# One hand-written work list of a convolution and SwiGLU kernel: a split sum and a tap of VectorE moved behind a step that they stood ahead of, and ten stores moved forward

## The chip, the cores and the metric

The kernel runs on one core of one Trainium2 chip. A core has four engines that compute, each with its own in-order list of instructions: TensorE (PE in the profile, its weight loads PEld), VectorE (DVE), ScalarE (ACT) and GpSimd (POOL). SyncE (SP) computes nothing; here it asks for nearly all DMA transfers, one after the other. The engines meet only through semaphores. The metric is device time in microseconds (us) of one execution, and the median over several runs is what counts.

## The reference

The computation has two layers, all in float32 (x comes in as float32, the weights as float64 words that the kernel converts itself):

```python
# x (8, 4096, 192), weight (8, 7): a causal depthwise convolution of 7 taps, one softmaxed filter per head of 24 columns
w = softmax(weight, axis=-1)
out[b, s, h, g] = sum_k w[h, k] * x_pad[b, s + k, h, g]
# then, on the 32768 rows of 192 columns:
xn  = x / sqrt(mean(x * x) + 1e-6) * rms_g
g   = xn @ w_gate            # 192 x 1536
val = xn @ w_val             # 192 x 1536
y   = (g * sigmoid(g) * val) @ w_out   # 1536 x 192
```

## The kernel before

The 32768 rows are worked in 32 pairs (0 to 31) of 1024 tokens. From pair 2 on, one pair goes through these stages:

- Loads: SyncE brings x of the pair, one transfer a head (`Sld.h`, line 174), into the one buffer `xh`; a pair that starts a sequence has one more small transfer for the zeros ahead of it (line 178).
- Convolution: tap 0 is a scaled copy on ScalarE (`Acv0`, line 470), taps 1 to 6 are multiply-adds on VectorE (`Vcv1` to `Vcv6`, line 474). They all work in place on the one buffer `y`.
- Normalisation (`Asq`, `Vred`, `Gpow`, `Vbc`, `Gmul`), eight stores into a scratch tensor (`Spl`, line 1098) and transfers back in token order into `xb` (`Sft`, line 676).
- Splitting: `Vx`, `An`, `Vl`, `Vd` make block sums of the tokens and cut each of five operands into three parts of fewer bits (lines 868, 705, 854, 856). Word `Vd.4` makes the third part of the fifth operand.
- Gate and value products: 68 products (line 948), each of six matmuls of 64x512, with weights from a ring of 12 places that SyncE refills from DRAM (line 822), 48 refills a pair. Eleven places have the name `ring`, and the twelfth lies in `part`. A place is asked for again as soon as its last product has read it.
- Between them ScalarE takes the silu (`Ag`, line 1031), VectorE multiplies (`Vm`, line 1038) and adds accumulators in PSUM (`Vf`, line 1025).
- Output: 42 steps on TensorE (line 976) into three accumulators X, Y and Z. `VC21` and `VC22` (line 1055) add an accumulator to a copy of another; `VT11`, `VT12`, `VT21` and `VT22` (line 991, two transposes each) turn the four quarters into `o_sb`; ten transfers `Sst0.0` to `Sst1.4` (line 1087) store them, `Sst0` for the first half of the tokens and `Sst1` for the second. A store needs both quarters of its half. The ten have 96, 96, 128, 32 and 32 KB for each half, all in runs of 64 floats, which is 256 bytes.

Nothing plans this order when the kernel is built: it is written out by hand as lists of words. `run` (line 1301) goes through a list and issues each word on the engine that its first letter names (A, V, G, S); `p3` issues the next three entries of the pair's list `LINE` (products, then steps) on TensorE. A plus behind a word means the next pair, two the one after it, a minus the pair before. So each list joins the tail of one pair with the body of the next and with what is got ready for later pairs. `FIRST` (line 115) serves pair 1, `SECOND` (line 98) pair 2, and `ORDER` (line 81) each of the pairs 3 to 31. Each engine runs its instructions in the order in which they were issued, and SyncE is no exception: a transfer whose data or place isn't ready holds up every transfer behind it.

Around the joint of pairs 1 and 2 the words stand so. `FIRST` ends with `VC21 p1 Vh4.4`, then the split sum and the tap, `Vd.4+` (pair 2) and `Vcv4++` (pair 3). (`Vl.2+` between them issues nothing, since `FIRST` has the same word earlier and `ahead_done`, line 1316, leaves out the second.) `SECOND` begins with the first two products of pair 2, `VC22-` and `VT11-` of pair 1, and `p6-`: the last six steps of pair 1. These write into accumulator X, which `VC22-` reads, and so can't start before it. At its other end `SECOND` has `Acv0++ p1 VC22 Vd.4+ Vcv4++ p5 VC21`: tap 0 and tap 4 of pair 4 ahead of `VC21`, which frees the accumulator that the first product of pair 3 goes into.

Of the kernel before, what the change touches and what calls it, by code (L numbers as in the profile page):

```python
# [20 lines left out]
def kernel(  # L21
# [75 lines left out]
    )  # L97
    SECOND = (
# [15 lines left out]
    )  # L114
    FIRST = (
# [14 lines left out]
    )  # L130
    LINE = (
# [1223 lines left out]
```

## Time and profile before

| | |
|---|---|
| median of 3 runs | 2451.31 us (2450.36 to 2458.17) |
| the profiled execution's own time | 2452.15 us |
| its span on the core | 2450.4 us |
| PE busy | 2429.1 us (99% of the span) |
| DVE busy | 2090.1 us (85%) |
| mean DMA rate | 176 GB/s |

The profile holds one execution. Its page gives busy times; the view of waits says which engine stood idle and what ended it; the timeline lists instructions in order of time, neighbours of one kind merged; the chain of waits is the work that ended last, followed back; the view of windows gives busy time and granted TensorE clock between two times. In a timeline row stand the start, the length, the engine, the line of the kernel, the operation, out<-in, the shapes, the count and, in brackets, the idle time before it and what ended it. SPq rows are SyncE's issues of DMA transfers, with the time in which SyncE was held in them.

### The profile page before, as it was taken

Reading aid. Unit: us, or ns where it says so; the run is one execution under the profiler, and the core shown is the slowest. Engines: PE = TensorE matmul, PEld = TensorE weight load, DVE = VectorE, ACT = ScalarE, POOL = GpSimd, SP = SyncE. Lnnn points to the kernel's source line nnn. Section 1 sums busy time; section 2 is a strip of 40 time slices with the busy share of each in tenths; the row PEclk is TensorE's granted clock in tenths of the full one; section 3 lists DMA queues with packets and bytes.
Section 4 is the critical chain, followed back from the end, with each engine's and each line's share of the span. In section 5 each row is a group of like instructions: output and inputs, shape, how many; then the busy total and the mean of one; then the engine's idle time right before and its main releaser. Section 6 shows DMA issues by size and latency. Waiting matters only on the chain.

```text
span 2450.4 us, 69381 instructions
## 1 busy us (share of the span) xinstructions
PE 2429.1 (99%) x29136; PEld 1979.6 (81%) x29136; DVE 2090.1 (85%) x2702; ACT 1033.3 (42%) x1431; POOL 565.3 (23%) x482
## 2 busy tenths in 40 slices
PE   8999999999999999999999999999999999999998
PEld 5647788888888888888788888888888788888786
DVE  8688888898888899888898888898888998888974
ACT  6443344444444443444443444433444443444432
POOL 0542122211222211222212222112222112222111
PEclk9999999999999999999999999999999999999999
DMA  7374688777787677787677786777786777876753
GB/s 153 61 212 133 156 197 207 180 170 174 173 205 198 172 179 172 174 214 194 167 178 168 184 213 185 171 176 171 190 210 183 170 174 174 198 201 177 177 157 83
DMA packets 716392, 430.55 MB, mean 176 GB/s; under 512 B 510330, under 2 KB 702386, under 8 KB 716082
## 3 DMA queue, kind: packets, MB, share of 16 engines
q1 hardware_dynamic: 712336, 425.21, 70.9%
q8 instruction: 230, 3.77, 0.7%
q10 hardware_dynamic: 3746, 0.92, 0.2%
q14 instruction: 80, 0.66, 0.1%
HBM read 366.96 MB, written 58.98 MB: 174 GB/s over the span
## 4 chain that ended last, share of the span: by engine, by line
PE 95%; DMA 1%; DVE 1%; POOL 1%; SPq 1%; issue 0%; ACT 0%; DVEq 0%; ACTq 0%; POOLq 0%
PE ps L948 57%; PE ps L976 35%; PE ps L1135 2%; SPq L174 0%; PE ps L920 0%; DMA ht<-in_moe_w_val_dram 0%; POOL ht L1003 0%; POOL part L799 0%; DVE ht L1003 0%; DMA x<-in_x_dram 0%; DMA wd<-part 0%; DMA xh<-in_x_dram 0%; SPq L258 0%; DMA ht<-in_moe_w_gate_dram 0%; DVE y L474 0%
## 5 line engine op out<-in xcount | busy, mean ns | idle before, releaser
L948 PE MATMUL ps<-part,ring 64*128 64x512 f32 x11160 | 1307.8, 387 | 3.6 <-DVE tt L1055 3.6
L948 PEld LDWEIGHTS ps<-part,ring 64*128 64x128 f32 x11160 | 1117.0, 184 | 158.8 <-issue 6.3
L1031 ACT ACTIVATE tt<-ps 128x512 f32<-128x512 f32 x744 | 441.3, 598 | 685.4 <-PE ps L948 618.3
L1038 DVE TENSOR_TENSOR ht<-ps,tt 128x512 f32<-128x512 f32 x744 | 498.8, 687 | 209.5 <-ACT tt L1031 201.2
L976 PE MATMUL ps<-ht,wo_sb 128*32 128x384 f32 (+2 forms) x7272 | 429.4, 380 | 2.6 <-DVE tt L1055 2.5
L976 PE MATMUL ps<-ht,x 128*32 128x256 f32 (+2 forms) x6696 | 411.0, 379 | 0.4 <-POOL ht L1003 0.3
L976 PEld LDWEIGHTS ps<-ht,wo_sb 128*32 128x32 f32 x7272 | 319.0, 110 | 99.4 <-issue 12.5
L976 PEld LDWEIGHTS ps<-ht,x 128*32 128x32 f32 x6696 | 291.7, 110 | 88.2 <-issue 0.8
L474 DVE SCALAR_TENSOR_TENSOR y<-xh,tp,y 128x1536 f32<-128x1536 f32 x186 | 338.3, 1819 | 7.8 <-ACT y L470 7.5
L503 POOL TENSOR_SCALAR r<-r 128x8 f32<-128x8 f32 x31 | 6.1, 197 | 1436.2 <-DVE r L498 1436.0
L1025 DVE TENSOR_TENSOR ps<-ps,tt 128x1024 f32<-128x1024 f32 x210 | 258.7, 1232 | 37.7 <-ACT tt L705 24.9
L705 ACT COPY ps<-ps 128x1024 f32<-128x1024 f32 (+1 forms) x151 | 134.0, 887 | 277.1 <-PE ps L948 126.9
L1003 POOL TENSOR_TENSOR hs<-ht 128x512 f32<-128x512 f32 x120 | 155.2, 1294 | 169.1 <-DVE ht L1038 127.8
L705 ACT COPY tt<-ps 128x384 f32<-128x384 f32 (+1 forms) x182 | 151.6, 833 | 86.9 <-PE ps L976 76.8
L705 ACT CAST part<-tt 128x1024 fp32r<-128x1024 f32 x60 | 62.8, 1046 | 288.7 <-DVE tt L868 288.7
L1003 DVE TENSOR_TENSOR ht<-ht 128x512 f32<-128x512 f32 x252 | 169.7, 705 | 4.7 <-PE ps L976 4.6
L1003 POOL TENSOR_TENSOR ht<-ht 128x512 f32<-128x512 f32 x120 | 154.0, 1294 | 2.3
L976 PE MATMUL ps<-hs,x 128*32 128x128 f32 (+2 forms) x2232 | 143.9, 379 | 0.0
L948 PE MATMUL ps<-part,part 64*128 64x512 f32 x912 | 129.8, 386 | 0.0
L976 PEld LDWEIGHTS ps<-hs,x 128*32 128x32 f32 x2232 | 103.7, 110 | 25.5
L856 DVE SCALAR_TENSOR_TENSOR part<-part,xb 128x1024 fp32r<-128x1024 f32 x87 | 106.5, 1224 | 0.0
L854 DVE TENSOR_TENSOR part<-xb,part 128x1024 fp32r<-128x1024 f32 x87 | 103.9, 1223 | 0.0
(137 smaller groups left out, 1627.6 us busy)
## 6 DMA issues: line engine op xcount, KB each, us to landing
ring<-wd SPq DMA_DIRECT2D x1326, 192.0 KB
xb<-xd SPq DMA_DIRECT2D x60, 512.0 KB
xd<-xh SPq DMA_DIRECT2D x240, 96.0 KB
part<-wd SPq DMA_DIRECT2D x114, 192.0 KB
xh<-in_x_dram SPq DMA_DIRECT2D x192, 105.0 KB
xb<-xd SPq DMA_DIRECT2D x60, 256.0 KB
out_dram<-o_sb SPq DMA_DIRECT2D x126, 96.0 KB
out_dram<-o_sb SPq DMA_DIRECT2D x62, 128.0 KB
```

The lines of the kernel that those rows point to most:

```text
L474: nc.vector.scalar_tensor_tensor(out=y, in0=xk, scalar=w, in1=y, op0=ALU.mult, op1=ALU.add)
L503: nc.gpsimd.tensor_scalar(out=r, in0=r, scalar1=s / D, scalar2=s * 1e-6, op0=ALU.mult, op1=ALU.add)
L705: nc.scalar.copy(out=dst, in_=src)
L854: e.tensor_tensor(out=split_of(g, 1).bitcast(F32R), in0=src, in1=high, op=ALU.subtract)
L856: nc.vector.scalar_tensor_tensor(out=split_of(g, 2).bitcast(F32R), in0=high, scalar=1.0 + SPLIT, in1=src, op0=ALU.mult, op1=ALU.subtract,)
L948: nc.tensor.matmul(out=self.both(j, c)[:, h, :], lhsT=left[HALF[h]], rhs=right[HALF[h]], start=(first and q == 0), stop=True, skip_group_c ...
L976: nc.tensor.matmul(out=self.acc(b)[i * Q : (i + 1) * Q, at : at + n], lhsT=left, rhs=cols, start=fresh, stop=True, skip_group_check=True, ...
L1003: engine[eng].tensor_tensor(out=dst, in0=a, in1=b, op=op)
L1025: nc.vector.tensor_tensor(out=self.both(j, c), in0=self.both(j, "b"), in1=s5, op=ALU.add)
L1031: nc.scalar.activation(out=tt[:, t, :], in_=self.both(j, c)[:, 0, :], func=AF.Silu)
L1038: nc.vector.tensor_tensor(out=self.hv(j, "abcd".index(c)), in0=self.both(j, c)[:, 1, :], in1=tt[:, t, :], op=ALU.mult,)
L1135: nc.tensor.matmul(out=bank(h, bks[h])[:], lhsT=wf[HALF[h], AT[h][k], u * NF + f, :], rhs=xb[HALF[h], g, k, :], start=(k == 0), stop=(k == ...
```

## The change

Only the end of `FIRST` and the list `SECOND` change, so one joint and one pair out of 32. The split sum `Vd.4` of pair 2 goes from ahead of `VC22-` to behind `VT11-` and the word `p6-`. The tap `Vcv4` of pair 3 goes from the same place to behind the fifteenth product of pair 2, just ahead of `Vmb.1`. The word `Vl.2` goes along and issues nothing in either kernel. The ten stores of pair 1 were asked for behind products 13, 14, 15, 55, 57, 60, 61, 65, 65 and 65 of pair 2; now they are asked for behind products 4, 4, 4, 7, 8, 9, 11, 12, 15 and 17. On TensorE, ScalarE and GpSimd the order of instructions stays the same; VectorE has the two instructions moved, and SyncE the stores.

```diff
     SECOND = (
-        "p2 VC22- VT11- p6- VT22- VT21- Vcv5+ VT12- Af1.0 p2 Aga.1 p1 Vma.1 Vl.4 p1 Aga.0 p1",
-        "Af3.0 Vma.0 p4 Vf4.0 p1 Agb.1 p1 Sst0.4- p1 Sst0.2- p1 Sst1.4- Vmb.1 p2 Vf5.0 Agc.0",
+        "p2 Vl.2 VC22- VT11- p6- Vd.4 VT22- VT21- Vcv5+ VT12- Af1.0 p2 Aga.1 Sst0.4- Sst0.2-",
+        "Sst1.4- p1 Vma.1 Vl.4 p1 Aga.0 p1 Sst0.3- Af3.0 Vma.0 p1 Sst1.1- p1 Sst0.0- p2 Vf4.0",
+        "Sst0.1- p1 Agb.1 Sst1.0- p3 Vcv4+ Vmb.1 Sst1.2- p2 Vf5.0 Agc.0 Sst1.3- p1 Vmc.0",
...
-        "Sst0.3- Gh3.0 Spl.6+ Vmd.4 p1 Gh3.1 Vmb.4 p1 Sst1.1- p1 Sft.0+ Af3.5 Sft.2+ p1",
-        "Sft.4+ Gh1.2 p1 Sst0.0- p1 Vf4.5 Sld.4++ Sst0.1- p2 Sft.5+ Aga.5 Vma.5 Sld.3++ p1",
-        "Agc.3 p1 Vf5.5 Sst1.0- Gh3.3 Sst1.2- Gh1.4 Sst1.3- Vh3.2 p1 Sld.7++ Vmc.3 p2 Vf6.5",
+        "Vmd.3 p2 Gh1.0 Agc.4 Spl.3+ Vmc.4 p1 Spl.0+ Agd.4 p1 Af1.5 Gh1.3 Agb.4 Gh3.0 Spl.6+",
+        "Vmd.4 p1 Gh3.1 Vmb.4 p1 p1 Sft.0+ Af3.5 Sft.2+ p1 Sft.4+ Gh1.2 p1 p1 Vf4.5 Sld.4++",
+        "p2 Sft.5+ Aga.5 Vma.5 Sld.3++ p1 Agc.3 p1 Vf5.5 Gh3.3 Gh1.4 Vh3.2 p1 Sld.7++ Vmc.3",
...
     FIRST = (
...
-        "VC21 p1 Vh4.4 Vl.2+ Vd.4+ Vcv4++",
+        "VC21 p1 Vh4.4",
```

19 rows, old and new, of the table SECOND are left out of this document.

## The prediction

> **What bounds the kernel now.** I read the page first, then the waits of TensorE, then the timeline at the two longest ones, then the chain of waits and windows by pair.
>
> ```profile
> PE 2429.1 (99%) x29136; PEld 1979.6 (81%) x29136; DVE 2090.1 (85%) x2702; ACT 1033.3 (42%) x1431; POOL 565.3 (23%) x482
> PE ps L948 <- DVE tt L1055: 3.6, 1, 3.6
> PE ps L976 <- DVE tt L1055: 2.5, 1, 2.5
> PE ps L222 <- DMA tt<-in_weight_dram: 2.1, 1, 2.1
> ```
>
> TensorE is the bound: it is busy for 99% of the span, and in the whole span it waits longer than 2.1 us only twice, each time once and each time for line 1055, the sums `VC22` and `VC21`. Both lie in the stretch that `SECOND` orders. The other 29 pairs have no such wait, so only these two, and what hangs on them, are there to be won. The first:
>
> ```profile
> 208.49 1.66 PE L948 MATMUL ps<-part,ring 64*128 64x512 f32 x12
> 208.61 0.69 DVE L1003 TENSOR_TENSOR ht<-ht 128x512 f32<-128x512 f32 x1 [0.67 <-PE ps L976]
> 209.22 1.22 DVE L856 SCALAR_TENSOR_TENSOR part<-part,tt 128x1024 fp32r<-128x1024 f32 x1
> 210.36 1.81 DVE L474 SCALAR_TENSOR_TENSOR y<-xh,tp,y 128x1536 f32<-128x1536 f32 x1
> 212.09 0.55 DVE L1055 TENSOR_TENSOR tt<-ps,tt 128x384 f32<-128x384 f32 x1
> 212.56 0.64 DVE L991 STREAM_TRANSPOSE o_sb<-ps 128x256 f32<-128x256 f32 x2
> 212.69 4.11 PE L976 MATMUL ps<-ht,wo_sb 128*32 128x384 f32 x72 [2.53 <-DVE tt L1055]
> 216.73 8.47 PE L948 MATMUL ps<-part,ring 64*128 64x512 f32 x72
> 216.87 0.65 DVE L991 STREAM_TRANSPOSE o_sb<-ps 128x256 f32<-128x256 f32 x2 [0.94 <-PE ps L976]
> ```
>
> The reader is to see the queue on VectorE: `Vh4.4` ends, then come `Vd.4` (209.22), `Vcv4` (210.36) and only then `VC22` (212.09), while TensorE has done its two products by 210.15 and stands for 2.53 us. The second wait is at the joint of pairs 2 and 3, and the chain of waits shows what leads up to it:
>
> ```profile
> 278.65 0.89 SPq L174
> ...
> 284.09 4.71 DMA xh<-in_x_dram
> ...
> 289.06 1.58 ACT y L470
> 290.67 1.82 DVE y L474
> 292.49 0.48 DVE tt L1055
> 293.01 48.23 PE ps L948 x408
> ```
>
> SyncE asks for the last of the x loads of pair 4 at 284.09; it lands 4.71 us later, then tap 0, tap 4 and `VC21` follow one by one, and TensorE goes on at 293.01, 4.2 us after the landing. The windows show what that idle time brings behind it:
>
> ```profile
> 208.49:293.01 84.52, 78.35 (x986) 65.17 (x984) 66.40 (x87) 31.50 (x42) 16.48 (x14) 1.00 0.65 161
> 293.01:369.12 76.11, 76.00 (x912) 67.15 (x912) 65.44 (x83) 31.52 (x42) 16.48 (x14) 0.98 0.76 179
> 443.31:517.30 73.99, 73.99 (x915) 63.83 (x914) 64.76 (x83) 31.45 (x42) 16.47 (x14) 1.00 0.77 184
> 289.30:293.00 3.70, 0.07 (x2) 0.00 (x0) 2.33 (x3) 1.34 (x1) 0.00 (x0) 1.00 0.00 0
> 293.30:296.70 3.40, 3.40 (x18) 2.68 (x18) 3.40 (x6) 1.00 (x1) 0.00 (x0) 0.50 0.22 58
> ```
>
> The first three are whole pairs, from the first product of one to that of the next; the third number from the right is the granted clock. An undisturbed pair takes 73.99 us. Pair 3 takes 76.11: it has no wait inside, but right behind the 3.64 us of idleness the clock is 0.50 for 3.4 us. So the second wait costs 3.64 and then another 2.1. Behind the 2.53 us wait the clock stays at 1.00.
>
> **The first two edits: `Vd.4` and `Vcv4` from ahead of `VC22`.** Without them `VC22` starts when `Vh4.4` lets go of VectorE, at 209.22. From its start to TensorE's it took 212.69 - 212.09 = 0.60 us, so the six steps are free at 209.82. TensorE's products end at 210.15. The wait goes whole, with 0.33 us to spare: -2.53.
>
> What is late next? `Vd.4` follows the two transposes of `VT11` and ends near 211.4; its reader is the thirteenth product, ten products of 0.7 (8.47 for twelve) behind the six steps, so near 221: some 9 us of cover hide it. `VT12` waits for the six steps (the 0.94 us above); VectorE has 1.14 us more to do ahead of it, so it comes 0.2 us later behind them, and an accumulator free that much later is hidden by ScalarE's copy and the products ahead of its next use. For `Vcv4`'s new place the trace has a stand-in: in pair 3 another tap stands there (301.89), between the sum `Vf4.0` and the multiply `Vmb.1`.
>
> ```profile
> 301.89 1.81 DVE L474 SCALAR_TENSOR_TENSOR y<-xh,tp,y 128x1536 f32<-128x1536 f32 x1
> 223.83 0.69 DVE L1038 TENSOR_TENSOR ht<-ps,tt 128x512 f32<-128x512 f32 x1 [1.07 <-ACT tt L1031]
> 225.24 1.23 DVE L1025 TENSOR_TENSOR ps<-ps,tt 128x1024 f32<-128x1024 f32 x1 [0.72 <-PE ps L948]
> 227.97 0.69 DVE L1038 TENSOR_TENSOR ht<-ps,tt 128x512 f32<-128x512 f32 x1 [0.73 <-ACT tt L1031]
> ```
>
> Pair 3 has no TensorE wait there. In pair 2 the same stretch has 1.07 + 0.72 + 0.73 = 2.52 us of VectorE idleness, more than the tap's 1.81. Its price lies between 0 and 1.81 (no cover at all); I take 0, from the pair that does it.
>
> **The ten stores.** Where they stood:
>
> ```profile
> 224.97 0.38 SPq L1087 DMA_DIRECT2D out_dram<-o_sb  x1
> 226.46 1.33 SPq L1087 DMA_DIRECT2D out_dram<-o_sb  x2
> 228.63 0.32 SPq L822 DMA_DIRECT2D part<-wd  x1
> 254.63 2.05 SPq L1087 DMA_DIRECT2D out_dram<-o_sb  x1
> 258.47 0.42 SPq L1087 DMA_DIRECT2D out_dram<-o_sb  x1
> 262.25 0.45 SPq L1087 DMA_DIRECT2D out_dram<-o_sb  x1
> 264.42 2.24 SPq L1087 DMA_DIRECT2D out_dram<-o_sb  x1
> 273.57 2.44 SPq L1087 DMA_DIRECT2D out_dram<-o_sb  x3
> 281.77 3.16 SPq L174 DMA_DIRECT2D xh<-in_x_dram  x4
> DMA packets 633, 0.16 MB, mean 161 GB/s; under 512 B 630, under 2 KB 633, under 8 KB 633
> 235.92 0.86 PE L948 MATMUL ps<-part,part 64*128 64x512 f32 x6
> ```
>
> Seven of them hold SyncE for 2.05 + 0.42 + 0.45 + 2.24 + 2.44 = 7.60 us between 254 and 276, a stretch in which SyncE issues without a pause and at the end of which stand the x loads. Taken out, they bring those loads forward by at most 7.60. If the DMA engines are what holds SyncE, the gain is what these save: the seven move 32 + 4*96 + 128 + 32 = 576 KB, 2304 runs of 256 bytes; between 276 and 277, where such runs are nearly all there is, the trace counts 633 packets (the row above), so 2304/633 = 3.6 us. If the refills in between, which wait for TensorE, set SyncE's pace, it is 0; but its rows follow each other without a pause, so that end is far. SyncE is held in some issues (2.05 and 2.24 where a free one takes 0.38 to 0.45) and goes at its own pace in others, so both limits work in turn, and I take some 5.
>
> What is needed? TensorE reaches the joint 2.53 earlier, and SyncE's stream, tied to TensorE by the refills, comes earlier with it. For no wait at all the last x load must land 3.64 us earlier still. That is just the smaller of the two limits, so the second wait goes, or all but a few tenths of it: -3.64. Its half clock goes with it: -(76.11 - 73.99) = -2.1.
>
> At their new places the stores cost SyncE time among the refills. The three early ones took 0.38 and 0.67 each, so ten take 4 to 7 us, and in the 12 us of the first 17 products nine refills at 0.32 take 3 more: there is room. The first one also waits for `VT12`, near 215, when no refill is due: the next place is let go by the fifth product, after it. The tightest cover I can show is that of the twelfth place: asked for at 228.63, read by the product at 235.92, 7.3 us later, of which landing takes some of the 2 to 5 us that DMAs take here. That leaves 2 to 5 us for refills delayed by stores. I take 0 and keep 2 as the bad end.
>
> Sum: -2.53 - 3.64 - 2.1 = -8.3 us, from 2452.15 of this execution to 2443.9. The execution shown lies 0.84 above the median, so against 2451.31 it is 2443.0. Pair 2 took 84.52 - 73.99 = 10.5 us more than an undisturbed one, of which the six steps are 4.0 (212.69 to 216.73) and the two waits 6.2, so at most 0.3 more is to be had: own range 2442.0 to 2444.3.
>
> The Trainium skill (TensorE: Matmul & The Clock Gate, section Part 1: The HAM clock gate) says that the array falls to half clock once it was idle for a whole window of about 3.4 us, and is back after as long a busy one; the trace agrees, with 3.64 us idle, then 0.50 for 3.4 us, and no drop behind 2.53. By that rule even a remaining wait of 3 us would cost only itself.
>
> **The rivals.** First, the loads don't come early enough. For it speaks that the smaller limit, 3.6 us, is just what is needed, and that refills stand between the loads. A remaining wait of 1 to 2.5 us without half clock gives 2444.0 to 2445.5; if all of it stays, with the half clock, only the first 2.53 is won: 2448.8. Second, the first wait gets a successor, at `VT12` or at `Vcv4`'s new place, and up to 1.81 comes back: 2444.8. Pair 3 speaks against it. Third, the other side: the stores hold up the refills behind them. At the price of the late ones (2.05 and 2.24 each) ten take some 21 us; SyncE has 12 - 3 = 9 free in that stretch and the cover is about 4, so TensorE would stand for 8 us, with 2.1 of half clock behind it: 10.1 against a gain of 8.3, so 2453.1. It decides from about 2 us a store; a store at 2.7 us would make it 2460. Against it: early in pair 2 stores took 0.38 to 0.67, since no block transfers of tokens run there. The Trainium skill (DMA: Bandwidth & Descriptors, section Specifications) speaks for it: it asks for runs of at least 512 bytes, with a read-modify-write below; no run here separates that from the 633 packets a us.
>
> **How the numbers follow.** The forecast has 0.63, the late loads 0.25, a successor 0.06, held refills 0.06. What a measurement of this kernel can tell from no change is about 0.3%, 7.4 us, and the forecast is only 0.9 beyond it. Of the first case 0.61 is faster, and of the second 0.03, where less than 0.9 us of the wait stays; the rest of both and the third count as the same, as does 0.02 of the last, whose 0.04 above 2458.7 is slower: 0.64, 0.32 and 0.04. The range takes in the first three cases with a little scatter: 2441.4 to 2449.3.
>
> **What would show it.** First wait: no idle time of TensorE ahead of the steps near 210, and `VC22` right behind `Vh4.4`. Tap: `Vcv4` ahead of `Vmb.1` with no TensorE wait for the next pairs of products. Second: the x loads of pair 4 end near 279 on SyncE, no wait at the joint near 287, and a granted clock of 1.00 in pair 3, which then takes 74.0 us. The prediction is wrong if TensorE waits for a refill in the first 30 products, or if the wait for line 1055 stays with more than 1 us.

## The result, and the profile after

| | before | after |
|---|---|---|
| median of 11 runs, us | 2453.72 (2450.36 to 2458.50) | 2445.48 (2443.56 to 2449.13) |
| ratio of the two | | 0.9965, 95% interval 0.9956 to 0.9974 |
| profiled execution, us (span) | 2452.15 (2450.4) | 2447.03 (2445.2) |

The changed kernel is faster by 0.35%, just beyond the 0.3% that the prediction took for the least that a measurement of this kernel can tell from no change. Both intended waits are gone. The waits of the changed kernel have no line for 1055 any more, and a 2.6 us entry for line 1003, which lies ahead of pair 2 and has its own paragraph below. The first line here is from the page, the others are from the view of waits (columns: us in total, times, longest):

```profile
PE 2427.2 (99%) x29136; PEld 1978.5 (81%) x29136; DVE 2089.3 (85%) x2702; ACT 1034.0 (42%) x1431; POOL 565.7 (23%) x482
PE ps L976 <- DVE ht L1003: 2.6, 2, 1.4
PE ps L222 <- DMA tt<-in_weight_dram: 2.1, 1, 2.1
```

The timeline of the changed kernel at the joint of pairs 1 and 2:

```profile
210.05 1.65 PE L948 MATMUL ps<-part,ring 64*128 64x512 f32 x12
210.17 0.69 DVE L1003 TENSOR_TENSOR ht<-ht 128x512 f32<-128x512 f32 x1 [0.67 <-PE ps L976]
210.78 0.55 DVE L1055 TENSOR_TENSOR tt<-ps,tt 128x384 f32<-128x384 f32 x1
211.25 0.64 DVE L991 STREAM_TRANSPOSE o_sb<-ps 128x256 f32<-128x256 f32 x2
211.64 4.11 PE L976 MATMUL ps<-ht,wo_sb 128*32 128x384 f32 x72
211.81 1.18 DVE L856 SCALAR_TENSOR_TENSOR part<-part,tt 128x1024 fp32r<-128x1024 f32 x1
221.60 1.81 DVE L474 SCALAR_TENSOR_TENSOR y<-xh,tp,y 128x1536 f32<-128x1536 f32 x1
```

`VC22` (210.78) stands right behind `Vh4.4`, the six steps follow the two products at 211.64 with no idle time, and the split sum (211.81) and the tap (221.60) stand at their new places. The same execution's stores and last x loads on SyncE, and the start of pair 3:

```profile
216.49 1.72 SPq L1087 DMA_DIRECT2D out_dram<-o_sb  x3
...
226.94 1.32 SPq L1087 DMA_DIRECT2D out_dram<-o_sb  x2
...
274.99 3.17 SPq L174 DMA_DIRECT2D xh<-in_x_dram  x4
286.62 0.55 DVE L1055 TENSOR_TENSOR tt<-ps,tt 128x384 f32<-128x384 f32 x1
...
288.29 0.96 PE L948 MATMUL ps<-part,ring 64*128 64x512 f32 x6
```

The ten stores are asked for between 216.49 and 228.26. `VC21` (286.62) is done 1.1 us before TensorE comes to the product that needs it. The windows of the changed kernel, pairs 2 and 3 (columns as in the prediction, the third number from the right is the granted clock):

```profile
210.05:288.29 78.24, 78.24 (x987) 64.53 (x985) 67.26 (x87) 31.43 (x42) 16.53 (x14) 1.00 0.69 174
288.29:362.23 73.94, 73.94 (x915) 63.84 (x913) 64.76 (x83) 31.44 (x42) 16.52 (x14) 1.00 0.75 184
```

Against 84.52 and 76.11, pair 2 is 6.28 shorter and pair 3 2.17, together 8.45 us, where the prediction had 8.3. The two profiled executions differ by only 5.12 because this one lost 3.3 us elsewhere. 1.56 of it is lost before pair 2 begins (210.05 against 208.49), at two waits in a part of `FIRST` that the change doesn't touch:

```profile
194.80 1.51 PE L976 MATMUL ps<-ht,x 128*32 128x384 f32 x24 [1.35 <-DVE ht L1003]
197.57 1.81 PE L976 MATMUL ps<-ht,x 128*32 128x384 f32 x28 [1.26 <-DVE ht L1003]
```

The other thirteen profiles of this study, among them a second one of the changed kernel, start pair 2 between 207.64 and 208.94. The remaining 1.7 are stalls of 0.2 to 1 us at scattered places of the later pairs. Their cause isn't known.

### The profile page after: what moved, and what is told of

Same layout as the page of the kernel before. It is cut to its first block, busy times and chain, and to the rows that moved or that the text cites. A ratio compares the mean times of both kernels' runs of the same rounds, so it can differ in the third digit from the quotient of the medians.

```text
span 2445.2 us, 69382 instructions
## 1 busy us (share of the span) xinstructions
PE 2427.2 (99%) x29136; PEld 1978.5 (81%) x29136; DVE 2089.3 (85%) x2702; ACT 1034.0 (42%) x1431; POOL 565.7 (23%) x482
## 3 DMA queue, kind: packets, MB, share of 16 engines
q1 hardware_dynamic: 712336, 425.21, 70.7%
## 4 chain that ended last, share of the span: by engine, by line
PE 97%; DVE 1%; DMA 1%; SPq 1%; issue 0%; ACT 0%; DVEq 0%; ACTq 0%
PE ps L948 57%; PE ps L976 35%; PE ps L920 2%; PE ps L1135 2%; SPq L174 1%; DMA ht<-in_moe_w_val_dram 0%; DVE part L854 0%; DMA x<-in_x_dram 0%; DVE ht L1003 0%; DMA xh<-in_x_dram 0%; DMA ht<-in_moe_w_gate_dram 0%; SPq L258 0%; DVE part L856 0%; DVE y L474 0%; DVE ht L1038 0%
## 5 line engine op out<-in xcount | busy, mean ns | idle before, releaser
L976 PEld LDWEIGHTS ps<-ht,x 128*32 128x32 f32 x6696 | 298.4, 110 | 86.5 <-DVE ht L1003 3.2
L976 PE MATMUL ps<-hs,x 128*32 128x256 f32 (+2 forms) x2232 | 145.2, 379 | 0.0
```

The costliest lines, as they stand in the source:

```text
L976: nc.tensor.matmul(out=self.acc(b)[i * Q : (i + 1) * Q, at : at + n], lhsT=left, rhs=cols, start=fresh, stop=True, skip_group_check=True, ...
```

## The experiments

All the kernels below do the whole computation. Times in the table count from the first product of pair 2; "landing" is the arrival of the last x load of pair 4 as the trace has it. Pair 2 is the time to the first product of pair 3, pair 3 that from there to the first of pair 4.

| run | profiled us | pair 2 | pair 3 | landing | wait ahead of the six steps | wait at the joint | half clock |
|---|---|---|---|---|---|---|---|
| before | 2452.15 | 84.52 | 76.11 | 80.31 | 2.53 | 3.64 | behind the joint |
| b_again (before) | 2450.09 | 82.54 | 74.61 | 77.98 | 2.54 | 0 | in the six steps |
| after | 2447.03 | 78.24 | 73.94 | 70.69 | 0 | 0 | none |
| a_again (after) | 2443.75 | 78.20 | 73.95 | 70.62 | 0 | 0 | none |
| e1_vector | 2445.57 | 78.54 | 74.55 | 74.34 | 0 | 0.24 | none |
| e1_second (same) | 2443.72 | 78.80 | 74.51 | 74.59 | 0 | 0.50 | none |
| e2_stores | 2448.10 | 81.73 | 74.12 | 75.99 | 2.53 | 0 | none |
| e3_queue | 2450.54 | 84.49 | 74.25 | 80.02 | 2.54 | 0 | none |
| e4_last3 | 2447.75 | 82.54 | 74.01 | 77.67 | 2.53 | 0 | in the six steps |
| e5_tap | 2447.31 | 80.65 | 74.54 | 76.44 | 0.80 | 1.51 | none |
| e6_split | 2450.05 | 80.55 | 74.52 | 76.34 | 1.41 | 0.79 | none |
| e7_bunch | 2445.08 | 78.31 | 73.93 | 71.07 | 0 | 0 | none |
| e8_twotaps | 2446.88 | 79.65 | 73.94 | 72.64 | 0, but 1.09 later | 0 | none |
| e9_late10 | 2453.63 | 80.38 | 75.50 | 76.25 | 0 | 2.13 | behind the joint |

**Each half of the change alone.** e1_vector has the two moves on VectorE and the stores at their old places, e2_stores the reverse:

```diff
 # e1_vector: stores as before
-        "p2 VC22- VT11- p6- VT22- VT21- Vcv5+ ...      ... Sst1.4- Vmb.1 p2 Vf5.0 ..."
+        "p2 VC22- VT11- p6- Vd.4 VT22- VT21- Vcv5+ ... ... Sst1.4- Vcv4+ Vmb.1 p2 Vf5.0 ..."
-        "VC21 p1 Vh4.4 Vl.2+ Vd.4+ Vcv4++",
+        "VC21 p1 Vh4.4",
 # e2_stores: FIRST as before, the stores at the changed kernel's places
-        "p2 VC22- VT11- p6- VT22- VT21- Vcv5+ VT12- Af1.0 p2 Aga.1 p1 ..."
+        "p2 VC22- VT11- p6- VT22- VT21- Vcv5+ VT12- Af1.0 p2 Sst0.4- Sst0.2- Sst1.4- Aga.1 p1 ..."
```

> The two edits on VectorE alone; the ten stores stay where they were. Pair 2 (from its first product to that of pair 3) was 84.52 us before and 78.23 after the whole change, pair 3 76.11 and 73.94. Theory (the terms add up, and SyncE's stream moves along with TensorE): the wait ahead of the six steps goes, pair 2 takes 81.9 us, the wait at the joint of pairs 2 and 3 stays at 3.6 us with half clock behind it, pair 3 stays at 76.1; 2.5 us faster in all. Rival (SyncE's stream sets its own pace): the loads land as late as before, the wait at the joint grows to 6.2 us, pair 2 stays at 84.5, no gain. A second rival: without the 2.5 us of idleness the loads find the joint a little better or worse, and the gain lies between 0 and 2.5.

> The ten stores alone at their new places; the split sum and the tap stay ahead of VC22. Theory (each wait has its own cause): the wait of 2.5 us ahead of the six steps stays, the one at the joint goes with its half clock; pair 2 takes 84.52 - 3.7 = 80.8 us, pair 3 74.0; 5.8 us faster in all. Rival (the whole gain hung on the VectorE edits, since the joint would be late anyway): the wait at the joint stays above 2 us. Here TensorE comes to the joint 2.5 us later than in the whole change, so the x loads have that much more room: if even here a wait stays, the stores weren't its cause.

In e1_vector the first wait is gone and the joint has 0.24 us left, where 3.6 were expected: the loads landed 6 us earlier than in the first profile of before. In e2_stores the first wait stays and the joint has none, as expected; its pair 2 is still 0.9 us over the expected 80.8, in one stall of TensorE in the output steps for which the profile names no releaser. Timed, e1_vector has a ratio of 0.9994 (0.9983 to 1.0004) and e2_stores 0.9994 (0.9986 to 1.0003), against a median of before of 2448.80 in that comparison, so neither half alone is told from no change, where 2.5 and 5.8 us had been expected. A second profile of e1_vector's kernel:

> The VectorE edits alone, a second profile. In the first the last x load landed 74.34 us behind the first product of pair 2, the wait at the joint was 0.24 us, pair 2 took 78.54. Theory (without the move of the stores the landing stands at the edge and varies by some 2 us from one execution to the next): landing between 73.5 and 77.5, wait between 0 and 3.3 us. Rival (the VectorE edits alone settle the joint): landing below 74 and no wait.

It shows 0.50 us at the joint and a landing within 0.3 us of the first, so both profiles of this kernel have a small remainder, and neither the scatter of 2 us nor the rival's landing below 74 was seen. The chain of waits of e1_vector, from the last x loads on, shows that the joint still hangs on them:

```profile
278.53 0.85 SPq L174
279.38 0.04 issue
279.42 3.52 DMA xh<-in_x_dram
...
283.20 1.58 ACT y L470
284.79 0.03 issue
284.81 1.82 DVE y L474
286.63 0.48 DVE tt L1055
287.11 0.04 issue
287.15 9.00 PE ps L948 x73
```

From the landing (282.94) to TensorE it is 4.21 us, as in before. Wherever TensorE waits here, it goes on 4.1 to 4.2 us after the landing: 80.38 against 76.25 in e9_late10, 80.65 against 76.44 in e5_tap.

**Both kernels profiled and the changed one timed again.**

> The changed kernel once more, beside the kernel before on one chip. First comparison: 2445.48 against 2453.72 us, ratio 0.9965. Beside the VectorE edits alone and the stores alone, the kernel before had a median of 2448.8 (2445.5 to 2458.2). Theory (the gain of the profile, 8.3 us, holds for every execution): ratio 0.9965 again. Rival (the wait at the joint is a matter of chance in the kernel before: with the VectorE edits alone the loads landed 6 us earlier and the wait was 0.24 us): the changed kernel takes 2445 to 2446 as it did, the kernel before 2448 to 2451, ratio 0.9980 to 0.9990.

> The kernel before, a second profile. Theory (the wait at the joint belongs to this order of stores): the last x load of pair 4 lands 80 us behind the first product of pair 2 (80.31 in the first profile), the wait is 3 to 4 us with half clock behind it, pair 2 takes 84 to 85 us and pair 3 76.1. Rival (chance): landing between 76 and 80, wait between 0 and 3 us, pair 2 between 80.8 and 84, pair 3 74.0 to 74.3. In both the wait ahead of the six steps is 2.53 us, since the order on VectorE makes it.

a_again has a median of 2444.76 against 2451.54, ratio 0.9974 (0.9965 to 0.9983), which lies between what the theory and the rival had expected, and its pairs 2 and 3 repeat those of the first profile within 0.03. b_again doesn't repeat before: its landing and its missing wait are those of the rival. The windows of that second execution of the kernel before, the last two lines being its first wait and what follows:

```profile
208.06:290.60 82.54, 80.00 (x986) 68.29 (x984) 66.75 (x87) 31.52 (x42) 16.46 (x14) 0.98 0.64 165
290.60:365.21 74.61, 74.56 (x914) 60.77 (x912) 65.58 (x83) 31.56 (x42) 16.49 (x14) 1.00 0.76 182
209.89:212.43 2.54, 0.17 (x4) 0.16 (x8) 2.54 (x4) 0.00 (x0) 0.00 (x0) 1.00 0.28 77
212.50:215.80 3.30, 3.30 (x36) 2.55 (x32) 3.00 (x7) 1.00 (x1) 0.00 (x0) 0.50 0.02 5
```

Here the half clock follows the first wait, and the joint has no wait at all. The six steps, 4.11 us before, took 5.79 (timeline of the same execution):

```profile
212.26 5.79 PE L976 MATMUL ps<-ht,wo_sb 128*32 128x384 f32 x72 [2.54 <-DVE tt L1055]
```

So TensorE came 1.7 us later to the joint, and the loads landed 2.3 earlier (77.98): 4.0 against the wait of 3.64.

**Which of the two VectorE moves.** e5_tap moves only `Vcv4`, e6_split only `Vd.4`. The lines show where the word goes from; in `SECOND` it stands at the changed kernel's place:

```diff
 # e5_tap
-        "VC21 p1 Vh4.4 Vl.2+ Vd.4+ Vcv4++",
+        "VC21 p1 Vh4.4 Vd.4+",
 # e6_split
-        "VC21 p1 Vh4.4 Vl.2+ Vd.4+ Vcv4++",
+        "VC21 p1 Vh4.4 Vcv4++",
```

> Of the change only the tap moved; the split sum stays ahead of VC22 and the stores at their old places. Theory (the wait ahead of the six steps is the time of what VectorE has in front of VC22): the tap took 212.09 - 210.36 = 1.73 us of it, so the wait falls from 2.53 to 0.80 us. At most 0.80 of one window of 3.41 us is idle, 23%; half clock has followed windows idle for 62% or more and none of 49% or less, so none follows here. Rival (VC22 waits for something else as well, the last steps into X or a copy by ScalarE): the wait stays above 1.2 us.

> Of the change only the split sum moved; the tap stays ahead of VC22 and the stores at their old places. Theory: the split sum took 210.36 - 209.22 = 1.14 us ahead of VC22, so the wait ahead of the six steps falls from 2.53 to 1.39 us, at most 41% of a window, and no half clock follows. Rival (moved behind the two transposes, the split sum holds up the turns and the tap behind them, and VT12 comes late for the products): a new TensorE wait within the next 12 products.

The waits of e5_tap over the whole execution (in the first row the longest, 1.5, is the one at the joint):

```profile
PE ps L948 <- DVE tt L1055: 2.2, 3, 1.5
PE ps L976 <- DVE tt L1055: 0.8, 1, 0.8
```

and of e6_split:

```profile
PE ps L976 <- DVE tt L1055: 1.4, 1, 1.4
```

Taking the tap away leaves 0.80, taking the split sum away 1.41, both away nothing: the first wait is VectorE's queue, and its terms add up.

**How much the tap's new place covers.** e8_twotaps puts a second tap there:

```diff
-        "... p3 Vcv4+ Vmb.1 Sst1.2- ...   ... Agb.0 p1 Vcv6+ Vmb.0 Vmd.0 ..."
+        "... p3 Vcv4+ Vcv6+ Vmb.1 Sst1.2- ...   ... Agb.0 p1 Vmb.0 Vmd.0 ..."
```

> The changed kernel with a second tap, Vcv6, brought forward to stand beside Vcv4 ahead of the multiply Vmb.1: 3.5 us of VectorE in that place instead of 1.75. Theory (the cover of the place is the 2.52 us of VectorE idleness in the stretch): the multiply comes 2.4 us late instead of 0.7, later work makes up 1.5 of it, and TensorE waits 0.5 to 1.5 us for line 1038 or 1025 near 15 us behind the first product; pair 2 78.7 to 79.7. Rival (accumulators free ahead of need add to the cover): no wait, 78.2. Where the cover is smaller than the prediction had it, the wait is 2 us or more.

The timeline of e8_twotaps:

```profile
219.79 3.66 DVE L474 SCALAR_TENSOR_TENSOR y<-xh,tp,y 128x1536 f32<-128x1536 f32 x2
...
225.44 0.98 PE L948 MATMUL ps<-part,ring 64*128 64x512 f32 x6 [1.09 <-DVE ps L1025]
```

Two taps, 3.66 us, make TensorE wait 1.09 us for the sum at line 1025. So one tap is free there because some 2.6 us of cover stand against its 1.81, not because the place costs nothing.

**Stores close together.** e7_bunch takes the changed kernel and asks for all ten stores behind product 4:

```diff
-        "... Af1.0 p2 Aga.1 Sst0.4- Sst0.2-", "Sst1.4- p1 ... Sst0.3- ... Sst1.3- ..."
+        "... Af1.0 p2 Sst0.4- Sst0.2- Sst1.4- Sst0.3- Sst1.1- Sst0.0- Sst0.1- Sst1.0- Sst1.2- Sst1.3- Aga.1 p1 ..."
```

> The changed kernel with all ten stores behind the fourth product of pair 2, in one row, ahead of every refill but the first. In the changed kernel they take SyncE 0.34 to 0.67 each and 1.0 to 1.3 a pair of them. Theory (refills have 2 to 5 us of cover): ten stores take 5 to 7 us of SyncE in one row from the end of the last transpose, the refills that come due in the 6 us meanwhile go out up to 5 us late; TensorE waits 0 to 2 us for a weight, pair 2 78.2 to 80.2. Rival of the prediction (held refills cost in full): a wait of 5 us or more for a DMA, with half clock behind it, pair 2 above 83.

SyncE's rows of e7_bunch:

```profile
214.87 5.64 SPq L1087 DMA_DIRECT2D out_dram<-o_sb  x10
220.61 4.97 SPq L822 DMA_DIRECT2D ring<-wd  x9
```

Ten stores in a row hold SyncE for 5.64 us, 0.56 each on average, the refills follow, and TensorE waits for none of them: pair 2 takes 78.31.

**What the late stores cost the loads.** e4_last3 moves only the last three (`Sst1.0`, `Sst1.2`, `Sst1.3`, to behind product 17). e3_queue leaves all at their places but lets ScalarE ask for the seven late ones. e9_late10 is e1_vector with all ten behind product 65.

```diff
 # e4_last3
-        "Agc.3 p1 Vf5.5 Sst1.0- Gh3.3 Sst1.2- Gh1.4 Sst1.3- Vh3.2 ..."
+        "... Vmb.1 p2 Sst1.0- Sst1.2- Sst1.3- Vf5.0 ...   Agc.3 p1 Vf5.5 Gh3.3 Gh1.4 Vh3.2 ..."
 # e3_queue: the same, also for Sst0.1, Sst1.0, Sst1.2 and Sst1.3
-        "Sst0.3- Gh3.0 Spl.6+ ... p1 Sst1.1- p1 ...", "... p1 Sst0.0- p1 ..."
+        "Ast0.3- Gh3.0 Spl.6+ ... p1 Ast1.1- p1 ...", "... p1 Ast0.0- p1 ..."
 # e9_late10
+        "Vma.5 Sld.3++ p1 Agc.3 p1 Sst0.4- Sst0.2- Sst1.4- Sst0.3- Sst1.1- Sst0.0- Sst0.1- Sst1.0- Sst1.2- Sst1.3- Vf5.5 ..."
```

> The kernel before, with only the last three late stores (Sst1.0, Sst1.2, Sst1.3: 256 KB, 2.44 us of SyncE) moved, to behind the seventeenth product. Theory (each store moved gives back its own issue time or its own engine time): the x loads land 1.6 (1024 runs at 633 a us) to 2.44 us earlier, the wait at the joint is 1.2 to 2.0 us, and no half clock follows, since the wait of 2.5 us ahead of the six steps isn't followed by one either: pair 2 82.1 to 82.9, pair 3 74.0. Rival (the early four, issued while SyncE is held by the full engines, are what counts): the wait stays above 3 us and pair 3 at 76.1. Rival on the clock (any wait of more than about 1 us is followed by half clock): pair 3 above 75 with a short wait.

> The kernel before, with the seven late stores at their old places in the list but asked for by ScalarE instead of SyncE. The bytes and the DMA engines' work stay where they were; only SyncE is freed of the 7.6 us that these stores held it. Theory (SyncE's issuing holds up the x loads): the loads come up to 7.6 us earlier, the wait at the joint goes, pair 2 takes about 80.8 us and pair 3 74.0. Rival (the DMA engines hold them up, and SyncE stands in its issues only because these are full): the loads land where they did, the wait stays at 2.5 to 3.6 us, pair 2 takes 83.4 to 84.5. Half and half: a wait of 1 to 2.5 us.

> The VectorE edits, with all ten stores in the worst place, behind product 65, between the transfers of tokens and the x loads. With the VectorE edits alone (three stores early, seven late) the last x load landed 74.34 us behind the first product and left a wait of 0.24 us. Theory (the stores' runs of 256 bytes on the DMA engines hold up the x loads behind them): three more stores, 192 KB or 768 runs at 633 a us, and the four that stood apart now come together: landing at 75.5 to 77.5, wait at the joint 1.4 to 3.4 us, pair 2 79.7 to 81.7. Rival (their place among the late transfers makes no difference): landing within 1 us of 74.3, wait under 1 us.

e4_last3 has no wait at the joint, but the half clock behind its first wait, as b_again. Its loads landed at 77.67 against 77.98 and 80.31 in the two executions of before, so its gain isn't told from their scatter. In e3_queue SyncE has no late store to issue, and still the loads land at 80.02, no earlier. But this doesn't answer the question that it was made for. The stores on ScalarE's queue, then SyncE's waits between 250 and 262 us in e3_queue:

```profile
253.05 0.84 ACTq L1087 DMA_DIRECT2D out_dram<-o_sb  x2
253.96 1.78 ACTq L1087 DMA_DIRECT2D out_dram<-o_sb  x2
257.81 1.89 ACTq L1087 DMA_DIRECT2D out_dram<-o_sb  x3
```

```profile
SPq L822 <- DMA out_dram<-o_sb: 5.0, 1, 5.0
SPq L1098 <- DMA out_dram<-o_sb: 1.6, 1, 1.6
```

SyncE is not freed here: by this view a refill (line 822) waits 5.0 us for such a store to land, and a transfer into the scratch tensor (line 1098) 1.6 us, while before has no wait of SyncE for a store in that stretch. (The timeline merges two refills into one row of 5.70 us there; each was asked for in 0.33.) These 6.6 us come in the place of the 7.6 that the issues had taken, and the first x load is asked for 58.0 us into the pair against 54.9 in before. TensorE has three waits in this pair that before hasn't (1.38, 0.71 and 0.3 us) and comes later to the joint, which is why the late landing makes no wait there. So it stays open how much of the loads' delay is SyncE's time in the issues and how much the DMA engines' work. In e9_late10 a wait of 2.13 us comes back at the joint, as its theory had it, with half clock behind it (windows):

```profile
207.64:288.02 80.38, 78.25 (x986) 62.82 (x984) 66.30 (x87) 31.50 (x42) 16.47 (x14) 1.00 0.69 169
288.02:363.52 75.50, 75.50 (x912) 61.05 (x912) 66.01 (x83) 31.41 (x42) 16.48 (x14) 0.98 0.72 180
288.20:291.50 3.30, 3.30 (x16) 2.61 (x18) 3.30 (x6) 1.00 (x1) 0.00 (x0) 0.50 0.20 59
```

The later the stores, the later the landing: with the same VectorE order it is 70.6 to 70.7 with all early, 74.3 to 74.6 at the old places, 76.25 with all ten late, and there it makes the wait. The rest of e9_late10's execution was also 4 to 8 us longer than the others', in scattered waits that are not explained.

## Why the prediction was right, and where its steps were off

The forecast was 2443.0 in a range of 2441.4 to 2449.3; measured were 2445.48 and, the second time, 2444.76. Its main case happened, and both profiles of the changed kernel show it. The gain was forecast as 8.3 us; the medians differ by 8.2 in the first comparison and by 6.8 in the second. In pairs 2 and 3 the changed kernel's second profile is 8.5 us shorter than the first profile of before and 5.0 shorter than b_again. So that the first comparison came out at 8.2 is partly luck.

- **First wait, -2.53: right.** The steps were to be ready 0.33 us ahead of TensorE; in the trace `VC22` started at 210.78, so by the prediction's 0.60 at 211.38, and TensorE began at 211.64: 0.26 spare. e5_tap and e6_split confirm the terms one by one: 2.53 - 0.80 = 1.73 for the tap, 2.53 - 1.41 = 1.12 for the split sum.
- **The tap's new place, 0: right, and for the reason given.** The idle time of 2.52 us that was named as cover is what e8_twotaps measured from the other side: 3.66 - 1.09 = 2.57. The rival of a successor wait there did not come about.
- **The joint, -3.64: right against the profiled execution, but not a part of every execution.** The step that failed is the one that took it for one. b_again has no wait there. It is 4.0 us away from the other profile of the same kernel: 1.7 is its half clock, 2.3 the landing. Of these 2.3, SyncE's issues are 0.8, since it was done with the last x load 76.44 us into the pair in the first profile and 75.63 in b_again; the other 1.5 are one late part of that load (last section). In the first profile two stores held SyncE for 2.05 and 2.24 us; in b_again SyncE came to the first of them 1.8 us later in the pair and was held 0.46 there:

```profile
255.95 0.46 SPq L1087 DMA_DIRECT2D out_dram<-o_sb  x1
...
264.54 1.91 SPq L1087 DMA_DIRECT2D out_dram<-o_sb  x1
```

- **Loads "some 5" us earlier: mis-sized.** With the VectorE moves in both, the stores' move brings the landing from 74.34 and 74.59 to 70.69 and 70.62, which is 3.7 to 4.0: near the 3.6 reckoned from the engines' packets, not the 7.6 of SyncE's time. In the old VectorE order it is 75.99 in e2_stores against 77.98 and 80.31, which is 2.0 to 4.3. The prediction needed 3.64 and called that "just the smaller of the two limits". It was enough, because of a thing that it put into half a sentence: SyncE's stream did come earlier with TensorE (80.31 and 77.98 in before, 74.34 and 74.59 in e1_vector), by more than the 2.53; why by more isn't shown. Each half of the change nearly ends the wait at the joint by itself: 0.24 and 0.50 us are left with the VectorE moves, none with the stores. Both together leave a margin: TensorE needs the landing 4.2 ahead of 78.2, so at 74.0, and has it 3.3 to 3.4 before that.
- **The half clock, -2.1: near in sum, wrong in the reason why it fell there, and too large.** Up to the first output step pair 3 took 48.17 us in before and 46.50 in the changed kernel, so the half clock cost 1.7. The other 0.5 of the 2.1 came in the output steps (27.94 against 27.44), where the clock was 1.00 again, and b_again has nearly as much there (27.89) without a half clock in its pair 3. "No drop behind 2.53" was the luck of one execution: of the five profiles with that wait two have the half clock behind it (b_again, e4_last3). What the change takes away is therefore a half clock at one of two places, in the six steps or in pair 3, worth 1.7 us at either, in both profiles of before; in how many executions wasn't counted.
- **Held refills: fell.** This rival needed 2 us a store; ten in a row took 0.56 each (e7_bunch). (Its 2460 at 2.7 us a store is 2459 from the median that the other sums start from.)
- **Pair 3, 74.0: right,** but there was a term that the sum didn't have. In the four profiles with a short wait at the joint and no half clock behind it (e1_vector, e1_second, e5_tap, e6_split) pair 3 takes 74.5 to 74.6 without any visible wait inside. In e1_vector TensorE begins pair 3 right at the end of `VC21` (287.11), in the changed kernel 1.1 us after it, so VectorE's work for the first products comes that much later. The waits of weight loads (PEld) in e1_vector's first 16 us of pair 3, which the changed kernel doesn't have:

```profile
PEld ps L948 <- DVE ps L1025: 0.6, 2, 0.3
PEld ps L948 <- DVE tt L1055: 0.5, 1, 0.5
PEld ps L948 <- DVE ht L1038: 0.3, 1, 0.3
```

Of those 1.4 us 0.6 show in the pair's time.

Two things stay open. The halves of the change measured 0.06% each and the whole 0.26% to 0.35%. That fits a first wait, a joint and a half clock of which each half removes one and leaves the others in part of the executions, but the frequencies weren't counted; and the medians of before itself lay between 2448.80 and 2453.72 in the three comparisons, of which at least two ran on different chips. Second, by which way the late stores hold up the loads: the 3.7 to 4.0 fit the DMA engines' 3.6, and no run separates these from SyncE's time.

## What to carry to other kernels

A wait that one profile shows at the end of a long DMA stream may be there in part of the executions only; profile the kernel before a second time ahead of putting its whole length into a sum. When several instructions stand ahead of the one that TensorE waits for, their durations add, and the cover at a new place can be read from the idle time of the engine there, to a tenth of a us here. Transfers that nobody is waiting for cost little at the head of a pair and hold the urgent ones at its tail, and when ScalarE asked for them here, SyncE waited for their landing instead. A row that merges several issues can hide such a wait, so the view of waits belongs beside it.

## What the runs showed of the hardware that was not expected

The half clock goes by fixed windows, not by the length of the wait. In each of the 14 traces the changes of the granted clock, from its first rise to its fall at the end, lie whole multiples of 3.413 us apart, and a half-clock stretch between them lasts 3.41 us. If such a change falls on the end of a window, it can be worked out how much of each window TensorE stood idle:

| wait | length, us | largest idle share of one window | clock behind it |
|---|---|---|---|
| before, at the joint | 3.64 | 92% | 0.50 |
| b_again, first wait | 2.54 | 74% | 0.50 |
| e4_last3, first wait | 2.53 | 63% | 0.50 |
| e9_late10, at the joint | 2.13 | 62% | 0.50 |
| e3_queue, first wait | 2.54 | 49% | 1.00 |
| e2_stores, first wait | 2.53 | 40% | 1.00 |
| before, first wait | 2.53 | 39% | 1.00 |

The same wait of 2.5 us lay mostly in one window in b_again and e4_last3 and was split more evenly over two in the last three rows. The limit lies between 49% and 62% of a window here: 1.67 us in one window weren't enough, 2.13 were. The windows of e4_last3 and e2_stores right behind the same 2.53 us:

```profile
213.45:216.70 3.25, 3.25 (x38) 2.36 (x32) 1.87 (x2) 0.24 (x1) 0.00 (x0) 0.50 0.00 0
```

```profile
212.80:216.20 3.40, 3.37 (x64) 2.79 (x68) 3.27 (x7) 1.00 (x1) 0.00 (x0) 1.00 0.02 5
```

The Trainium skill (TensorE: Matmul & The Clock Gate, section Part 1: The HAM clock gate) says that the windows of 3413 ns run freely; the multiples of 3.413 agree. It also wants a whole idle window for the drop, and the 2.13 us of e9_late10 contradict that: the prediction's sentence that a remaining wait of 3 us would cost only itself, by that rule, doesn't hold. The trace of before doesn't agree with that part either, though the prediction says so: its 3.64 us filled no window whole, but 92% of one.

In the first profile of before a transfer that no instruction of the kernel asks for runs beside the tail of the last x load: one packet of 0.02 MB on a queue that the profile calls "instruction". The DMA queues between 286 and 287 us, then the kernel's own queue between 286 and 289:

```profile
q1 hardware_dynamic: 947, 0.09, 70.4%
q8 instruction: 1, 0.02, 6.0%
q1 hardware_dynamic: 968, 0.09, 24.6%
```

The packet takes 6.0% of 16 engines' time in that us, so 0.96 us of one engine; in the trace it runs from 286.82 to 287.78. Only 21 of the kernel's packets are left behind 287, and the first of them starts at 287.76. Of the 16 arrivals that the trace records for the last x load 15 are in by 287.29, and the last comes at 288.81, 1.5 us later; in each of the other thirteen profiles the last is at most 0.6 us behind the one before it. So the likely reading is that one engine's part of the load stood behind that packet, and that the wait at the joint would have been some 2.1 us without it (an estimate, 3.64 - 1.52). One execution shows it, and no run tests it.
